# Matmuls of a constant in TensorE's waits, and a finer cut of the last weight, at the end of an attention-plus-FFN decode step

## The chip, the cores and the metric

The kernel runs on one core of one Trainium2 chip. The metric is the device time of one execution in microseconds; lower is better. Three runs of the kernel before gave 1332.01, 1332.43 and 1332.98 us, a median of 1332.43 us.

## The reference

Four sequences decode one token each. A modulation vector is made from `c`, then comes attention over a cache of 4096 keys and values for 32 heads of 128, then a feed-forward block:

```python
mod = (_silu(c) @ w_mod).reshape(4, 6, 1, -1)      # sa, ca, ga, sb, cb, gb
h = _layernorm(x) * (1 + ca) + sa
q = (h @ wq) per head;  scores = einsum(q, k_cache) * 128 ** -0.5
o = einsum(softmax(scores), v_cache)
x = x + ga * (o @ wo)
h = _layernorm(x) * (1 + cb) + sb
x = x + gb * (_silu(h @ w1) @ w2)                   # w1: 512 x 1792, w2: 1792 x 512
```

All values are float32. The two caches alone are 537 MB, and every byte of them is used once.

## The kernel before, in words

The work is cut into N = 64 steps: 16 pairs of heads (t) times 4 sequences (b). One step n loads 4 MB of keys and 4 MB of values into buffers that rotate through one pool of five (tag "kv"), which the weights `wo`, `w1` and `w2` use too. All these loads are issued by SyncE (line 71, in `fetch` and `load`), in the order in which the program writes them, so they stand in one queue.

In a step GpSimd and VectorE multiply the keys with the query (L216), VectorE sums them (L221) and takes the maximum (L225), TensorE transposes the maximum (L229), ScalarE takes the exponential into `pz` (L247), and TensorE multiplies `pz` with the values in `pv` (L260): 16 matmuls with 32 weight columns and 512 moving columns, of which four stand side by side on the four column groups of the array. The trace shows each of these as two instructions (32 in a step).

The schedule is manual: each engine does its instructions in the order of the program. The end of the kernel is this. In the last step (n = 63) SyncE is given the loads of the last values, of the second half of `wo` (four pieces, L319), of `w1` (three pieces, L334) and of `w2` (four pieces, L335). TensorE does the first half of the output projection, `project(0, NH)` (L336, matmuls on L294, 64 of them with 128 moving columns), and then `pv(63)` (L337), for which the last values must have landed. Then follow, one after the other and each waiting for the last:

- `finish_a` and `finish_b` (L340, L341): VectorE copies the sums (L269), TensorE reduces them (L271, L276), VectorE divides;
- `project(NH, NT)` (L342): 64 more matmuls on L294;
- `x1` and the layer norm on VectorE (L345 to L347), with two small matmuls (L165, L169) and one square root on ScalarE (L171) inside it, then the transpose `h2T` (L131);
- the first FFN matmul into `ph` (L352): for each of four slices k of `w1` four matmuls, one a column group, with 448 moving columns;
- SiLU: tanh on ScalarE (L126), a product on VectorE (L127) and the transpose `hidT` (L131);
- the second FFN matmul into `pf` (L362): 14 slices i of `w2`, four matmuls each with 128 moving columns;
- two products and sums on VectorE (L367, L368) and the store (L371).

`psum(..., "q", 2)` is a pair of PSUM banks that `make_qb` (L196) uses in turn for the spread queries; `ph` takes one of them. `ident` is a 128x128 identity, and `qs` holds the scaled queries, written once at the start.

Of the kernel before, what the change touches and what calls it, by code (L numbers as in the profile page):

```python
# [17 lines left out]
def kernel(  # L18
# [13 lines left out]
    nc = tc.nc  # L32
    P = 128
    B, H, S, Dh = kc.shape
    D = x.shape[2]
# [10 lines left out]
    NI = F // P  # L46
# [13 lines left out]
    def psum(shape, tag, bufs):  # L60
        return ps.tile(shape, F32, tag=tag, name=tag, bufs=bufs)
# [5 lines left out]
    w2v = w2.rearrange("(p i) d -> p i d", p=P)  # L67

    def fetch(t, src, *cuts):
        for lo, hi in zip(cuts, cuts[1:]):  # L70
            nc.sync.dma_start(t[:, lo:hi], src[:, lo:hi])

    def load(name, shape, src, *cuts):
        t = kv.tile(shape, F32, tag="kv", name=name)
        fetch(t, src, *(cuts or (0, shape[1])))
        return t
# [3 lines left out]
    def load_k(n):  # L80
        t, b = divmod(n, B)
        src = kc[b, HP * t : HP * (t + 1)].rearrange("h (p j) d -> (h p) j d", p=HALF)
        kt[n] = load(f"k{n}", [P, NJ, Dh], src)

    def load_v(n):
        t, b = divmod(n, B)
        src = vc[b, HP * t : HP * (t + 1)].rearrange("h (p j) d -> (h p) j d", p=HALF)
        vt[n] = load(f"v{n}", [P, NJ, Dh], src)
# [14 lines left out]
    ident = const.tile([P, P], F32, name="ident")  # L103
# [25 lines left out]
    def transposed(src, m, name):  # L129
        d = const.tile([P, m, W], F32, name=name)  # L130
        nc.vector.transpose(d, src.rearrange("p (c k) -> p k c", k=m))  # L131
        return d
# [23 lines left out]
    def layernorm_mod(dst, src, sh, sc1):  # L156
        def t(tag, n):
            return work.tile([P, n], F32, tag=tag, name=tag, bufs=1)

        st, mv, dm, q, r, u = t("st", 6), t("mv", 2), t("dm", 1), t("lnq", 1), t("lnr", 2), t("lnu", P)  # L160
        nc.vector.bn_stats(st, src)
        nc.vector.bn_aggr(mv, st)
        avgm = avg.rearrange("p g w -> p (g w)")
        pm = psum([P, 1], "mx", 2)
        nc.tensor.matmul(pm, avgm, mv[:, 0:1], start=True, stop=True)  # L165
        nc.vector.tensor_sub(dm, mv[:, 0:1], pm)
        nc.vector.scalar_tensor_tensor(q, dm, dm, mv[:, 1:2], op0=ALU.mult, op1=ALU.add)
        pq = psum([P, 1], "mx", 2)
        nc.tensor.matmul(pq, avgm, q, start=True, stop=True)  # L169
        nc.vector.scalar_tensor_tensor(u, src, pm, sc1, op0=ALU.subtract, op1=ALU.mult)  # L170
        nc.scalar.activation(r[:, 0:1], pq, AF.Sqrt, bias=epst)  # L171
        nc.vector.reciprocal(r[:, 1:2], r[:, 0:1])
        nc.vector.scalar_tensor_tensor(dst, u, r[:, 1:2], sh, op0=ALU.mult, op1=ALU.add)
# [7 lines left out]
    CW = 4 * Dh  # L181
    pq = [psum([P, CW], "q", 2) for _ in range(2)]
    for k in range(NK):
        for ch in range(H * Dh // CW):
# [3 lines left out]
                start=k == 0, stop=k == NK - 1,  # L188
            )
    qs = const.tile([P, 2, CW], F32, name="qs")  # L190
# [5 lines left out]
    def make_qb(t):  # L196
        p = psum([P, B, Dh], "q", 2)
        for b in range(B):
            for i in range(HP):
                ch, u = divmod(HP * t + i, CW // Dh)  # L200
                j, g = divmod(ch, G)
                nc.tensor.matmul(  # L202
                    p[HALF * i : HALF * (i + 1), b, :],
                    ident[:, W * g + b : W * g + b + 1].to_broadcast([P, HALF]),
                    qs[:, j, u * Dh : (u + 1) * Dh],
                    start=True, stop=True,
                )
        qb[t] = p
        qw[t] = work.tile([P, B, Dh], F32, tag="qw", name=f"qw{t}")
        nc.scalar.activation(qw[t], p, AF.Copy)  # L210
# [3 lines left out]
    def mult(eng, src, n, lo, hi):  # L214
        t, b = divmod(n, B)
        eng.tensor_mul(  # L216
            kt[n][:, lo:hi, :], kt[n][:, lo:hi, :], src[t][:, b : b + 1, :].to_broadcast([P, hi - lo, Dh])
        )

    def red(n, lo, hi):  # L220
        nc.vector.tensor_reduce(sc[n][:, lo:hi], kt[n][:, lo:hi, :], axis=AX.X, op=ALU.add)  # L221

    def rowmax(n):
        nm[n] = work.tile([P, 1], F32, tag="rm", name=f"rm{n}", bufs=3)
        nc.vector.tensor_reduce(nm[n], sc[n], axis=AX.X, op=ALU.max)  # L225
# [27 lines left out]
    def pv(n):  # L253
        t, b = divmod(n, B)
        if b == 0:
            po[t] = psum([P, JJ * Dh], "po", 2)
        o = W // 2 - JJ - JJ * b
        for j in range(NG):
            g = j % G
            nc.tensor.matmul(  # L260
                po[t][W * g : W * (g + 1), :],
                pz[n % NP][:, j * W + o : (j + 1) * W + o],
                vt[n][:, JJ * j : JJ * (j + 1), :].rearrange("p j d -> p (j d)"),
                start=(b == 0 and j < G), stop=(b == B - 1 and j >= NG - G),
            )

    def finish_a(t):
        o = work.tile([P, JJ, Dh], F32, tag="o", name="o")
        nc.vector.tensor_copy(o, po[t].rearrange("p (j d) -> p j d", j=JJ))  # L269
        d = psum([P, 1 + HP, B], "small", 1)  # L270
        nc.tensor.matmul(d[:, 0, :], blk, rs[t], start=True, stop=True)  # L271
        for i in range(HP):
            for r in range(HP):
                for j in range(JJ):
                    s = i * W // 2 + j
                    nc.tensor.matmul(  # L276
                        d[HALF * i : HALF * (i + 1), 1 + r, :], o[:, j, r::HP], sel[:, s : s + JJ * (B - 1) + 1 : JJ],
                        start=j == 0, stop=j == JJ - 1,
                    )
        sm[t] = d  # L280

    def finish_b(t):
        rd = work.tile([P, 1, B], F32, tag="rd", name="rd")
        nc.vector.reciprocal(rd, sm[t][:, 0:1, :])
        nc.vector.tensor_mul(oz[:, t, :, :B], sm[t][:, 1 : 1 + HP, :], rd.to_broadcast([P, HP, B]))  # L285
# [4 lines left out]
    def project(lo, hi):  # L290
        for t in range(lo, hi):
            for r in range(HP):
                for g in range(G):
                    nc.tensor.matmul(  # L294
                        accp[W * g : W * (g + 1), :], oz[:, t, r, :],
                        wot[t // NH][:, t % NH, r, g * P : (g + 1) * P],
                        start=(t == 0 and r == 0), stop=(t == NT - 1 and r == HP - 1),
                    )

    NH = NT // 2  # L300
    make_qb(0)
    load_v(0)
    for n in range(N):
        t, b = divmod(n, B)
        if n + 1 < N - 3:
            load_k(n + 1)
            load_v(n + 1)
        elif n == N - 4:
            load_k(N - 3)
            load_k(N - 2)  # L310
            load_k(N - 1)
        elif n == N - 3:
            load_v(N - 3)
            load_v(N - 2)
        elif n == N - 2:
            wot.append(load("wo0", [P, NH, HP, D], wov[:, :NH]))
        else:
            load_v(n)
            wot.append(load("wo1", [P, NH, HP, D], wov[:, NH:], 0, NH // 2, 3 * NH // 4, NH - 1, NH))  # L319
        sc[n] = work.tile([P, NJ], F32, tag="sc", name=f"sc{n}", bufs=3)  # L320
        mult(nc.gpsimd, qw, n, 0, NA)
        mult(nc.vector, qb, n, NA, NJ)
        if n >= B and b == 0:
            finish_a(t - 1)
        red(n, NA, NJ)
        if n >= B and b == 0:
            finish_b(t - 1)
        red(n, 0, NA)
        rowmax(n)
        bmax(n)  # L330
        negmax(n)
        softexp(n)
        if n == N - 1:
            w1t = load("w1", [P, NK, F], w1v, 0, 2, 3, 4)  # L334
            w2t = load("w2", [P, NI, D], w2v, 0, 8, 12, 13, 14)  # L335
            project(0, NH)  # L336
        pv(n)  # L337
        if b == 1 and t + 1 < NT:
            make_qb(t + 1)
    finish_a(NT - 1)  # L340
    finish_b(NT - 1)  # L341
    project(NH, NT)  # L342

    x1 = const.tile([P, P], F32, name="x1")
    nc.vector.tensor_mul(x1, ga, accp)  # L345
    nc.vector.tensor_add(x1, x1, xg)
    layernorm_mod(hg, x1, sb, cb1)  # L347
    h2T = transposed(hg, NK, "h2T")
    ph = psum([P, FG], "q", 2)
    for k in range(NK):  # L350
        for g in range(G):
            nc.tensor.matmul(  # L352
                ph[W * g : W * (g + 1), :], h2T[:, k, :], w1t[:, k, g * FG : (g + 1) * FG],
                start=k == 0, stop=k == NK - 1,
            )
    hid = const.tile([P, FG], F32, name="hid")
    silu2(hid, ph, FG)
    hidT = transposed(hid, NI, "hidT")
    pf = psum([P, P], "po", 2)
    for i in range(NI):  # L360
        for g in range(G):
            nc.tensor.matmul(  # L362
                pf[W * g : W * (g + 1), :], hidT[:, i, :], w2t[:, i, g * P : (g + 1) * P],
                start=i == 0, stop=i == NI - 1,
# [32 lines left out]
```

## Time and profile before

| what | us |
|---|---|
| median of three runs (lowest, highest) | 1332.43 (1332.01, 1332.98) |
| the profiled execution | 1334.54 |
| span of the profiled execution, first to last instruction | 1332.5 |
| VectorE busy in it | 976.2 (73%) |
| TensorE matmuls busy | 504.9 (38%) |
| GpSimd busy | 435.2 (33%) |
| ScalarE busy | 75.7 (6%) |
| DMA rate over the span | 426 GB/s |

The profile is of one execution. "PE" is TensorE's matmuls, "PEld" its weight loads, which lie beside them, "DVE" is VectorE, "ACT" ScalarE, "SPq" the queue of SyncE that issues DMAs. The granted clock (PEclk) is the share of full speed that TensorE was given in a stretch: 1.0 is 2.4 GHz and 0.50 is 1.2 GHz, and a value between them is a stretch with some of each. Ends of matmuls are modelled, starts are recorded. A few matmul records can be missing.

### The profile page before, as it was taken

What the parts mean: (1) busy time and instruction counts of PE and PEld (TensorE: products, weight loads), DVE (VectorE), ACT (ScalarE), POOL (GpSimd) and SP (SyncE); (2) the same over time, 40 slices, a digit from 0 to 9 for tenths busy, and PEclk for the clock granted to TensorE, in tenths of its full rate; (3) what the DMA queues carried; (4) which work ended last, traced back from release to release, by engine and by line L of the source; (5) the groups of instructions that cost most, each with busy time, mean ns of one, the idle gap of its engine ahead of it and who ended that gap; (6) DMA issues with size and microseconds to landing.
All of it is one profiled execution on the core that took longest, in us unless ns stands there. A gap on an engine that the chain in (4) does not pass through costs nothing.

```text
span 1332.5 us, 8833 instructions
## 1 busy us (share of the span) xinstructions
PE 504.9 (38%) x3576; PEld 181.2 (14%) x3576; DVE 976.2 (73%) x468; ACT 75.7 (6%) x289; POOL 435.2 (33%) x79
## 2 busy tenths in 40 slices
PE   3244324433442533443343233334333333433157
PEld 2011101110110111101011110101111011101024
DVE  1487787788778778777877877777787787778851
ACT  1100000000000000000000000000000000000000
POOL 1244234324323423432442343243234234324600
PEclk9666677666656666656666676576666556666677
DMA  9999999999999999999999999999999999999997
GB/s 407 427 430 433 426 436 428 429 435 426 433 432 429 433 427 435 430 430 432 427 435 429 428 434 429 432 430 431 432 429 430 430 432 432 431 428 433 431 414 288
DMA packets 22376, 567.87 MB, mean 426 GB/s; under 512 B 2448, under 2 KB 2496, under 8 KB 5056
## 3 DMA queue, kind: packets, MB, share of 16 engines
q1 hardware_dynamic: 22160, 567.29, 99.3%
q8 instruction: 28, 0.46, 0.1%
q14 instruction: 12, 0.10, 0.0%
q0 software_dynamic: 128, 0.01, 0.0%
q10 hardware_dynamic: 48, 0.01, 0.0%
HBM read 567.30 MB, written 0.01 MB: 426 GB/s over the span
## 4 chain that ended last, share of the span: by engine, by line
DMA 48%; DVE 35%; PE 10%; issue 4%; ACT 2%; DVEq 0%; ACTq 0%
DMA k<-in_A_k_cache_dram 45%; DVE sc L221 20%; DVE k L216 13%; PE po L260 8%; DMA v<-in_A_v_cache_dram 2%; ACT pz L247 2%; PE mx L229 1%; DMA wm<-in_w_mod_dram 1%; DVE o L269 1%; DVE rm L225 1%; DVE nm L236 1%; PE acc L294 0%; PE po L362 0%; PE q L352 0%; DVE oz L285 0%
## 5 line engine op out<-in xcount | busy, mean ns | idle before, releaser
L216 POOL TENSOR_TENSOR k<-k,qw 128x3072 f32<-128x3072 f32 x64 | 429.7, 6715 | 827.9 <-DMA k<-in_A_k_cache_dram 786.7
L221 DVE TENSOR_REDUCE sc<-k 128x40 f32<-128x5120 f32 (+1 forms) x128 | 560.8, 4413 | 5.2
L216 DVE TENSOR_TENSOR k<-k,q 128x5120 f32<-128x5120 f32 x64 | 351.2, 5488 | 245.9 <-DMA k<-in_A_k_cache_dram 188.2
L260 PE MATMUL po<-v,pz 128*32 128x512 f32 x2048 | 371.5, 892 | 103.0 <-ACT pz L247 77.1
L229 PE MATMUL mx<-ident,rm 128*128 128x128 f32 x64 | 28.5, 445 | 641.4 <-DVE rm L225 641.4
L260 PEld LDWEIGHTS po<-v,pz 128*32 128x32 f32 x2048 | 82.6, 155 | 349.0 <-issue 256.3
L247 ACT ACTIVATE pz<-sc,nm 64x64 f32<-64x64 f32 x128 | 44.2, 345 | 1054.1 <-DVE nm L236 1052.5
L229 PEld LDWEIGHTS mx<-ident,rm 128*128 128x128 f32 x64 | 11.6, 181 | 676.2 <-issue 648.2
L236 DVE TENSOR_REDUCE nm<-mx 64x1 f32<-64x64 f32 x128 | 28.4, 222 | 45.9 <-PE mx L229 43.9
L276 PE MATMUL small<-sel,o 128*64 128x4 f32 x512 | 43.0, 231 | 46.6 <-DVE o L269 46.6
L276 PEld LDWEIGHTS small<-sel,o 128*64 128x64 f32 x512 | 41.6, 190 | 48.0 <-DVE o L269 48.0
L247 ACT ACTIVATION_READ_ACCUMULATOR pz<-sc,nm 64x1 f32 x128 | 23.6, 185 | 0.0
L269 DVE COPY o<-po 128x512 f32<-128x512 f32 x16 | 11.0, 684 | 16.2 <-PE po L260 16.2
L202 PE MATMUL q<-qs,ident 128*64 128x128 f32 x256 | 17.5, 279 | 0.0
L225 DVE TENSOR_REDUCE rm<-sc 128x1 f32<-128x64 f32 x64 | 14.1, 220 | 2.2
L202 PEld LDWEIGHTS q<-qs,ident 128*64 128x64 f32 x256 | 13.6, 136 | 14.5 <-issue 14.5
L210 ACT ACTIVATE qw<-q 128x512 f32<-128x512 f32 x16 | 9.6, 597 | 105.5 <-PE q L202 105.5
L146 PE MATMUL q<-wm,csT 128*32 128x128 f32 x192 | 7.5, 322 | 17.2 <-DVE csT L131 13.5
L186 PE MATMUL q<-wq,hT 128*32 128x512 f32 x64 | 10.1, 790 | 9.5 <-DMA wq<-in_A_wq_dram 9.5
L294 PE MATMUL acc<-wo,oz 128*32 128x128 f32 x256 | 11.7, 369 | 0.4 <-DMA wo<-in_A_wo_dram 0.4
L294 PEld LDWEIGHTS acc<-wo,oz 128*32 128x32 f32 x256 | 11.2, 154 | 0.7 <-issue 0.6
L146 PEld LDWEIGHTS q<-wm,csT 128*32 128x32 f32 x192 | 6.2, 129 | 17.9 <-DVE csT L131 13.5
(57 smaller groups left out, 63.8 us busy)
## 6 DMA issues: line engine op xcount, KB each, us to landing
k<-in_A_k_cache_dram SPq DMA_DIRECT2D x64, 4096.0 KB, 36.0
v<-in_A_v_cache_dram SPq DMA_DIRECT2D x64, 4096.0 KB, 30.3
wq<-in_A_wq_dram SPq DMA_DIRECT2D x2, 4096.0 KB
wm<-in_w_mod_dram SPq DMA_DIRECT2D x2, 3072.0 KB, 10.1
wo<-in_A_wo_dram SPq DMA_DIRECT2D x1, 4096.0 KB
wo<-in_A_wo_dram SPq DMA_DIRECT2D x1, 2048.0 KB
w<-in_B_w_dram SPq DMA_DIRECT2D x1, 2048.0 KB, 23.7
w<-in_B_w_dram SPq DMA_DIRECT2D x1, 1792.0 KB
```

Of the source, the lines that this page charges most:

```text
L146: nc.tensor.matmul(p[W * g : W * (g + 1), u, :], csT[:, k, :], wmt[k // 2][:, k % 2, o : o + P], start=k == 0, stop=k == NK - 1,)
L202: nc.tensor.matmul(p[HALF * i : HALF * (i + 1), b, :], ident[:, W * g + b : W * g + b + 1].to_broadcast([P, HALF]), qs[:, j, u * Dh : (u + ...
L216: eng.tensor_mul(kt[n][:, lo:hi, :], kt[n][:, lo:hi, :], src[t][:, b : b + 1, :].to_broadcast([P, hi - lo, Dh]))
L221: nc.vector.tensor_reduce(sc[n][:, lo:hi], kt[n][:, lo:hi, :], axis=AX.X, op=ALU.add)
L225: nc.vector.tensor_reduce(nm[n], sc[n], axis=AX.X, op=ALU.max)
L229: nc.tensor.transpose(p, nm[n].to_broadcast([P, P]), ident)
L236: nc.vector.tensor_reduce(t[h], nm[n][h, h], axis=AX.X, op=ALU.max, negate=True)
L247: nc.scalar.activation(w[:, :, o + i * W // 2 : o + i * W // 2 + JJ], sc[n][h].rearrange("p (g j) -> p g j", j=JJ), AF.Exp, bias=nm[n][h], ...
L260: nc.tensor.matmul(po[t][W * g : W * (g + 1), :], pz[n % NP][:, j * W + o : (j + 1) * W + o], vt[n][:, JJ * j : JJ * (j + 1), :].rearrange ...
L269: nc.vector.tensor_copy(o, po[t].rearrange("p (j d) -> p j d", j=JJ))
L276: nc.tensor.matmul(d[HALF * i : HALF * (i + 1), 1 + r, :], o[:, j, r::HP], sel[:, s : s + JJ * (B - 1) + 1 : JJ], start=j == 0, stop=j == ...
L294: nc.tensor.matmul(accp[W * g : W * (g + 1), :], oz[:, t, r, :], wot[t // NH][:, t % NH, r, g * P : (g + 1) * P], start=(t == 0 and r == 0 ...
```

## The change

A helper `busy(m)` issues m matmuls that multiply the first half of `qs` (128 x 512) with the whole identity into a PSUM tile of its own, `idle`, which nobody reads. Nineteen of them are put at six places of the end: 6 between the first half of the projection and `pv(63)`, 2 before the second layer norm, 3 behind it, 2 behind slice 1 and 2 behind slice 2 of the first FFN matmul, and 4 between the two FFN matmuls. The load of `w2` is cut at other slices: 0, 4, 8, 11, 13, 14, which makes five pieces (six numbers), where there were four.

```diff
     NH = NT // 2
+    idle = []
+
+    def busy(m):
+        if not idle:
+            idle.append(psum([P, CW], "q", 2))
+        for _ in range(m):
+            nc.tensor.matmul(idle[0], ident, qs[:, 0, :], start=True, stop=True)
+
     make_qb(0)
...
         if n == N - 1:
             w1t = load("w1", [P, NK, F], w1v, 0, 2, 3, 4)
-            w2t = load("w2", [P, NI, D], w2v, 0, 8, 12, 13, 14)
+            w2t = load("w2", [P, NI, D], w2v, 0, 4, 8, 11, 13, 14)
             project(0, NH)
+            busy(6)
         pv(n)
...
     nc.vector.tensor_add(x1, x1, xg)
+    busy(2)
     layernorm_mod(hg, x1, sb, cb1)
     h2T = transposed(hg, NK, "h2T")
+    busy(3)
     ph = psum([P, FG], "q", 2)
     for k in range(NK):
         for g in range(G):
...
                 start=k == 0, stop=k == NK - 1,
             )
+        if k in (1, 2):
+            busy(2)
+    busy(4)
     hid = const.tile([P, FG], F32, name="hid")
```

## Rows read from the trace of the kernel before

**Rows 1.** The chain that ended last, in order of time: start, us, what.

```profile
1267.96 30.29 DMA v<-in_A_v_cache_dram
...
1305.74 1.88 PE small L276 x32
...
1329.16 0.30 DVE y L367
```

**Rows 2.** The end by stretches: us, busy time of each engine, PEclk, DMA share, GB/s.

```profile
1288.60:1294.90 6.30, 6.30 (x128) 6.06 (x128) 0.15 (x1) 2.14 (x5) 0.00 (x0) 0.57 0.98 415
1294.90:1298.39 3.49, 0.03 (x4) 0.03 (x1) 0.00 (x0) 0.00 (x0) 0.00 (x0) 0.87 0.91 365
1298.39:1305.00 6.61, 6.61 (x34) 1.72 (x34) 0.01 (x1) 0.00 (x0) 0.00 (x0) 0.55 1.04 417
...
1307.55:1312.92 5.37, 5.36 (x130) 5.09 (x128) 0.35 (x2) 0.00 (x0) 0.00 (x0) 0.68 1.03 428
...
1316.96:1321.87 4.91, 4.91 (x32) 1.29 (x32) 0.00 (x0) 0.23 (x1) 0.00 (x0) 0.65 0.79 325
...
1324.16:1329.10 4.94, 4.93 (x112) 4.64 (x112) 0.00 (x0) 0.00 (x0) 0.00 (x0) 0.65 0.05 18
1329.10:1332.50 3.40, 0.00 (x0) 0.00 (x0) 0.58 (x2) 0.00 (x0) 0.00 (x0) 0.87 0.01 2
```

**Rows 3.** Timeline of TensorE's matmuls: start, us, what, idle time before and its releaser.

```profile
1298.39 6.54 PE L260 MATMUL po<-v,pz 128*32 128x512 f32 x32 [3.46 <-DMA v<-in_A_v_cache_dram]
...
1314.29 0.35 PE L165 MATMUL mx<-mv,avg 128*128 128x1 f32 x2 [1.37 <-DVE mv L162]
...
1316.96 4.91 PE L352 MATMUL q<-w,h2T 128*32 128x448 f32 x32 [1.37 <-DVE h2T L131]
1324.16 4.93 PE L362 MATMUL po<-w,hidT 128*32 128x128 f32 x112 [2.29 <-DVE hidT L131]
```

**Rows 4.** Timeline, weight loads of two earlier and later pv steps: one row each four.

```profile
1270.77 0.13 PEld L260 LDWEIGHTS po<-v,pz 128*32 128x32 f32 x4 [0.29 <-issue]
1271.20 0.13 PEld L260 LDWEIGHTS po<-v,pz 128*32 128x32 f32 x4 [0.30 <-issue]
...
1300.07 0.23 PEld L260 LDWEIGHTS po<-v,pz 128*32 128x32 f32 x4 [0.62 <-issue]
1300.92 0.23 PEld L260 LDWEIGHTS po<-v,pz 128*32 128x32 f32 x4 [0.62 <-issue]
```

**Rows 5.** Groups of instructions by line and form, whole execution: busy us, mean ns.

```profile
L260 PE MATMUL po<-v,pz 128*32 128x512 f32 x2048 | 371.5, 892 | 103.0 <-ACT pz L247 77.1 <-DMA v<-in_A_v_cache_dram 21.9 <-issue 4.0
L229 PE MATMUL mx<-ident,rm 128*128 128x128 f32 x64 | 28.5, 445 | 641.4 <-DVE rm L225 641.4
L202 PE MATMUL q<-qs,ident 128*64 128x128 f32 x256 | 17.5, 279 | 0.0
L271 PEld LDWEIGHTS small<-rs,blk 128*128 128x128 f32 x32 | 4.8, 188 | 14.5 <-issue 14.5
```

**Rows 6.** SyncE's issues of the weights w1 and w2 between 1296 and 1300 us.

```profile
L71 SPq DMA_DIRECT2D w<-in_B_w_dram x3: 856/1172/1175, 1295.5 to 1298.3; - x3
```

**Rows 7.** DMA issues of the same stretch: KB each, us from issue to landing.

```profile
w<-in_B_w_dram SPq DMA_DIRECT2D x1, 2048.0 KB, 23.7
w<-in_B_w_dram SPq DMA_DIRECT2D x2, 896.0 KB
```

**Rows 8.** The DMA's last microseconds, by stretches as in rows 2.

```profile
1325.00:1326.00 1.00, 1.00 (x26) 0.99 (x22) 0.00 (x0) 0.00 (x0) 0.00 (x0) 0.50 0.10 33
1326.00:1327.00 1.00, 1.00 (x25) 0.99 (x20) 0.00 (x0) 0.00 (x0) 0.00 (x0) 0.50 0.00 0
```

**Rows 9.** Timeline of all engines: SyncE's weight issues, and VectorE's last use of `q`.

```profile
1273.04 5.49 DVE L216 TENSOR_TENSOR k<-k,q 128x5120 f32<-128x5120 f32 x1
...
1283.97 23.54 SPq L71 DMA_DIRECT2D w<-in_B_w_dram  x7
...
1329.80 0.67 SPq L371 DMA_DIRECT2D out_dram<-y  x2
```

## The prediction

> **What bounds the kernel now.** I read the page's slices of clock and DMA first: the DMA works at its rate until the last of the forty slices, so the time in front of the last values is a matter of bytes, and the change leaves the bytes alone. So I went to the chain that ended last, for what comes behind them. The last values land at 1298.25 us, 30.29 after 1267.96 [rows 1]; what TensorE and VectorE do after that, some 34 us, is the only part that the change can touch. Third, the end by stretches, for the clock: the last `pv` ran at a granted clock of 0.55, the second half of the projection at 0.68, and both FFN matmuls at 0.65 [rows 2]. The reader should see that each of these began at or fell to 1.2 GHz after TensorE had been idle or nearly so, and rose to 2.4 GHz after it had streamed for some time. Fourth, TensorE's timeline, for the idle time ahead of each stretch: 3.46 us for the values, 1.37 us ahead of the norm's first matmul, 1.37 us ahead of the first FFN matmul, 2.29 us ahead of the second [rows 3]. The change fills these.
>
> **What full clock can give back.** A stretch that streams all the time at a mean clock c would take c times its time at full clock, so it gives back (1 - c) of it [rows 2]: `pv` 6.61 x 0.45 = 2.97 us; the projection 5.37 x 0.32 = 1.72; the first FFN matmul 4.91 x 0.35 = 1.72; the second 4.94 x 0.35 = 1.73. Together 8.14 us. The 1.88 us of the reduction [rows 1] ran at full clock already and give nothing.
>
> **What one matmul of the constant costs.** The trace has none of 128 weight columns by 512 moving ones. The nearest in length is `pv`: its weight loads, four to a pass, come 0.43 us apart at full clock and 0.85 us apart at half [rows 4]. Four column groups share that pass; is a pass over the whole array as long? In L202 two groups share it, 16 passes of 128 columns in each of 16 calls (256 instructions), with 17.5/16 = 1.09 us a call, 0.137 us a pair [rows 5]; a pair of 512 columns would be four times that at most, 0.55. So neither two groups nor four makes a pass much shorter or longer, and I take 0.43. Every ordinary float32 matmul stands twice in the trace (8 matmuls a call, 16 instructions in L202), so one matmul of the constant is two passes: 0.85 us at full clock, 1.71 at half. The lower bound is one pass, 0.43: the transposes with the same identity are 64 instructions in 64 steps [rows 5]. The upper bound adds a weight load in the open to every pass: 0.188 us for 128 columns [rows 5], 1.23 us in all. I take 0.85, since `pv`'s loads lie beside the pass before.
>
> **What lies beside other work and what on the path.** TensorE does its instructions in order, so whatever of a fill lasts longer than the idle time delays the real matmul behind it, and the VectorE work behind that.
> - busy(6): 5.12 us where 3.46 were idle. It holds `pv` back, and with it the copy on VectorE: +1.66.
> - busy(2) ahead of the norm: 1.71 against 1.37, and the matmul of the means and its subtraction on VectorE wait: +0.34. `x1` itself does not wait, as it needs only the projection.
> - busy(3): 2.56 against 1.37; the first FFN matmul waits though `h2T` is there: +1.19.
> - busy(2) twice inside the first FFN matmul: no idle time stands between its slices (one row of 4.91 us busy in 4.91 [rows 2]), so all four matmuls are on the path: +3.41. This is the dearest item. It would cost nothing if `w1` were late there. But the first part of `w2`, 2048 KB, was issued at 1298.3 [rows 6] and landed 23.7 us later [rows 7], at 1322.0, and at 325 to 417 GB/s [rows 2] those bytes take 5.0 to 6.5 us, so the last of `w1`, ahead of it in the queue, landed at 1317 or before (an estimate). By the sums here, slice 2 is needed at about 1318.8 and slice 3 at 1321.2 in the changed kernel.
> - busy(4): 3.41 against 2.29 of SiLU; the second FFN matmul waits: +1.12.
>
> Sum of the fills 7.72 us, given back 8.14 us: **0.42 us faster than the profiled execution**, a span of 1332.1. The second FFN matmul would begin 1.3 us later than now (7.72 of fills less 2.97 + 1.72 + 1.72 given back), at about 1325.5, and take 1.73 less.
>
> **The pieces of w2.** They are five, not six. All 3.67 MB still follow `w1` in the one queue. The extra issue takes at most the 1.175 us of the longest in [rows 6]; SyncE has nothing to do from 1307.51 (1283.97 + 23.54) until the store at 1329.80 [rows 9], so this is hidden; without that cover it would cost itself. The first slices would be there about 2.5 us sooner (half of the 5.0), but the second FFN matmul waits for `hidT` [rows 3], not for them: 0. The last bytes land in the stretch from 1325 to 1326 [rows 8]; the last slice is needed at about 1328.4. That leaves 2 to 3 us, and this is what is late next if the path shrinks.
>
> **The PSUM bank.** `idle` takes the bank that `ph` had, last read for step 59; `ph` moves to the one that VectorE reads for step 63, from 1273.04 on for 5.49 us [rows 9], 38 us before `ph` needs it. No wait: 0; without that lead, at most those 5.49 us.
>
> **Against the median.** The profiled execution took 1334.54 us, 2.11 more than the median. The clock is a draw: all 64 `pv` steps have the same matmuls and took 371.5/64 = 5.80 us busy on average [rows 5], against 6.54 in the last [rows 3]. If none of the 2.11 us is a colder clock at the end, the sum stands, -0.42; if all of it is, the kernel before had 2.11 us less to give back in those runs, and the change costs +1.69. I take the middle, +0.6: **1333.0 us**. For this kernel a measurement can tell about 0.2% (2.7 us) from nothing, so this is no change.
>
> **The rivals.**
> - *The fills cost half or less.* If the matmul of the constant goes in one pass, as the transposes do, fills of 2.56, 0.85, 1.28 and 1.71 us fit inside their idle times, and only the two inside the first FFN matmul cost, 1.71 us. Then 6.4 us would be saved, but the last bytes of `w2` stop it: landed at about 1325.6, two short rounds of matmuls (0.2) and the end of 3.40 us [rows 2] give a span of 1329.2, 3.3 less. Against the median, with half of the 2.11 us gone, that is -2.2: 1330.2. For: the fills would fit the gaps closely. Against: every ordinary matmul of the trace has two passes. The Trainium skill (TensorE: Matmul & The Clock Gate, "Wait — 56ns, not 53.3ns?") gives 215.7 ns from start to start for 512 columns at full clock, in its own measurements; by that figure, an estimate, the nineteen take 4.1 us in all, four of them (0.86 us) on the path, and the time is this rival's. The rows here say 0.43 us a pass and two passes, so I give this little. Chance 0.12, of which 0.05 beyond 0.2%.
> - *Weight loads in the open: slower.* `pv` shows loads of 32 columns beside a running pass. If loads over all 128 columns can't start until the pass that uses the whole array is done, each of the 38 passes gets 0.188 us more [rows 5]: 7.1 us, all on the path, as the fills are longer than their cover already: 1333.0 + 7.1 = 1340.1. It decides from 0.055 us a pass on (2.1 us over 38). For: nothing in the trace loads a whole array beside a long pass. Against: `pv` loads the same column group while it streams, without a gap. Chance 0.08.
> - *The constant does not hold the clock.* Then nothing is given back and each matmul takes 1.71 us: 32.4 us less the covers of 8.49 is 24 us slower, 1356. Against: `pv` streams with weights that are mostly zero too, and the clock rises in it. Chance 0.03.
> - Something else: 0.04.
>
> **How the numbers follow.** My forecast has 0.73; its own range goes from -0.42, less 0.7 for the modelled ends of five idle times, to +1.69, plus about 1 if one stretch still starts cold: 1331.3 to 1335.1. The range over cases takes in most of the first rival: 1330.2 to 1335.6; the slower rivals, the rest and the edges, some 0.18, are left out. Faster by over 0.2%: 0.05 from the first rival and 0.02 from the forecast's edge, 0.07. Slower: 0.08 + 0.03 + 0.04 of edges and the rest, 0.15. Within: 0.78.
>
> **What would show it.** Right: from 1295 us on the granted clock stays near 1.0; fills with weight loads 0.43 us apart; `pv` starts about 1.7 us after its values landed and lasts 3.6 us; the first FFN matmul is split and lasts 6.6 us from start to end; no wait for `w1` or `w2`. Wrong: passes 0.2 us apart, or 0.6; a clock of 0.5 within the fills; a second FFN matmul that waits for the DMA; a SiLU that ends behind busy(4).

## The result, and the profile after

The changed kernel took 1336.38 us (median of 8 runs, 1335.77 to 1338.58), the kernel before in the same comparison 1332.62 us (8 runs, 1331.86 to 1333.43). The ratio is 1.003, with a 95% interval of 1.002 to 1.004: slower by 3.8 us, where no change was forecast, and 0.8 us above the stated range.

The clock did what was hoped. The end of the changed kernel by stretches, with the columns of [rows 2]: the fill ahead of `pv`, `pv`, the second half of the projection, the norm with its two fills, the first FFN matmul with its two, the fill behind it, and the second FFN matmul.

```profile
1295.05:1300.39 5.34, 5.34 (x14) 2.19 (x12) 0.00 (x0) 0.00 (x0) 0.00 (x0) 1.00 0.97 391
1300.39:1304.10 3.71, 3.71 (x35) 1.07 (x34) 0.00 (x0) 0.00 (x0) 0.00 (x0) 1.00 1.05 420
1306.65:1310.35 3.70, 3.70 (x131) 3.50 (x129) 0.35 (x2) 0.00 (x0) 0.00 (x0) 1.00 0.99 414
1310.35:1316.01 5.66, 5.07 (x18) 2.33 (x22) 2.62 (x10) 1.54 (x2) 0.00 (x0) 1.00 1.01 411
1316.01:1323.26 7.25, 7.25 (x41) 2.09 (x41) 0.00 (x0) 0.00 (x0) 0.00 (x0) 1.00 0.78 315
1323.26:1326.89 3.63, 3.63 (x12) 1.44 (x16) 1.56 (x2) 0.54 (x1) 0.00 (x0) 1.00 0.18 72
1326.89:1330.15 3.26, 3.19 (x112) 2.92 (x112) 0.00 (x1) 0.00 (x0) 0.00 (x0) 1.00 0.00 0
```

The granted clock is 1.00 throughout, where [rows 2] had 0.55 to 0.68. TensorE is busy for almost all of it, and that is the trouble: the chain that ended last, in order of time, now runs through the matmuls of the constant (L307).

```profile
1295.12 5.35 PE q L307 x12
1300.46 3.61 PE po L260 x32
...
1306.72 3.63 PE acc L294 x128
1310.35 1.91 PE q L307 x4
...
1313.33 2.68 PE q L307 x6
1316.01 1.64 PE q L363 x16
1317.65 1.91 PE q L307 x4
1319.56 0.89 PE q L363 x8
1320.45 1.91 PE q L307 x4
1322.37 0.89 PE q L363 x8
1323.26 3.63 PE q L307 x8
1326.89 3.24 PE po L376 x112
```

Four instructions of it (two matmuls) take 1.91 us, eight 3.63, twelve 5.35: 0.86 us a matmul, and 0.19 us once for each of these fills; the fill of three (2.68) has 0.10. The six fills sum to 17.39 us. In the profile of before the same chain went from the values to `pv` [rows 1] with none of this.

### The profile page after: what moved, and what is told of

Read it like the earlier page. It is cut to its first block, busy times and chain, and to the rows that moved or that the text cites. A ratio compares the mean times of both kernels' runs of the same rounds, so it can differ in the third digit from the quotient of the medians.

```text
span 1333.9 us, 8910 instructions
## 1 busy us (share of the span) xinstructions
PE 510.9 (38%) x3614; PEld 183.5 (14%) x3614; DVE 976.2 (73%) x468; ACT 75.7 (6%) x289; POOL 435.1 (33%) x79
## 4 chain that ended last, share of the span: by engine, by line
DMA 46%; DVE 36%; PE 11%; issue 5%; ACT 2%; DVEq 0%; ACTq 0%
DMA k<-in_A_k_cache_dram 43%; DVE sc L221 21%; DVE k L216 13%; PE po L260 7%; DMA v<-in_A_v_cache_dram 3%; ACT pz L247 2%; PE q L307 1%; PE mx L229 1%; DMA wm<-in_w_mod_dram 1%; DVE o L269 1%; PE acc L294 1%; DVE rm L225 1%; DVE nm L236 1%; PE q L363 0%; PE po L376 0%
## 5 line engine op out<-in xcount | busy, mean ns | idle before, releaser
L260 PE MATMUL po<-v,pz 128*32 128x512 f32 x2048 | 364.7, 877 | 99.0 <-ACT pz L247 77.1
L269 DVE COPY o<-po 128x512 f32<-128x512 f32 x16 | 10.9, 684 | 14.7 <-PE po L260 14.7
L307 PE MATMUL q<-qs,ident 128*128 128x512 f32 x38 | 17.9, 608 | 0.0
```

The lines of the kernel that those rows point to most:

```text
L260: nc.tensor.matmul(po[t][W * g : W * (g + 1), :], pz[n % NP][:, j * W + o : (j + 1) * W + o], vt[n][:, JJ * j : JJ * (j + 1), :].rearrange ...
L307: nc.tensor.matmul(idle[0], ident, qs[:, 0, :], start=True, stop=True)
```

## The experiments

All ratios are to the kernel before, run beside each kernel on the same chip. Its medians in the four comparisons lie between 1332.62 and 1333.20 us, so medians from different comparisons can be set side by side to some 0.6 us. Three theories stood: (1) the fills that outlast their waits are the loss, measured against a kernel before that in most executions had less to give back than in the profiled one; (2) the profiled execution of before is typical; (3) the cut of `w2`, or the longer program, costs.

### e1 and e11: the kernel before, two more profiles

No edit.

> The kernel before, unchanged, for a second profile of it. Theory 1 (the draw): the one profiled execution of before was colder at its end than most, so that the change had less to give back than it seemed. Then this profile spans about 1330.5 us (the median of 1332.6 less the 2.1 between time and span), and at least two of the four stretches (pv, the second half of the projection, the two FFN matmuls) have a granted clock well above the 0.55, 0.68, 0.65 and 0.65 of the first profile. Theory 2 (the draw is no part of it): the four clocks are within 0.05 of those, and the span is 1332 or more, or it is shorter for another reason.

> The kernel before, unchanged, for a third profile. Theory 1 (the clock of the end is drawn anew in each execution): a span between 1329.8 and 1332.5, and a set of four clocks unlike either of the first two profiles. Rival (the first profile was an odd one, the second is the rule): the four clocks within 0.05 of the second profile.

Measured: the second profile spans 1330.3 us (median of 10 runs 1332.35, ratio 0.9996, interval 0.9987 to 1.0005), the third 1329.4 (one run, 1331.47), 0.4 below the span that I had stated for it. The same stretches as [rows 2], the second profile and then the third: `pv`, projection, first and second FFN matmul.

```profile
1298.36:1303.52 5.16, 5.16 (x34) 1.42 (x34) 0.01 (x1) 0.00 (x0) 0.00 (x0) 0.71 1.04 414
1306.07:1309.84 3.77, 3.70 (x130) 3.43 (x128) 0.35 (x3) 0.00 (x0) 0.00 (x0) 1.00 1.01 421
1313.82:1318.72 4.90, 4.90 (x32) 1.11 (x32) 0.00 (x0) 0.22 (x1) 0.00 (x0) 0.65 1.01 420
1322.09:1326.90 4.81, 4.76 (x112) 4.50 (x112) 0.00 (x0) 0.00 (x0) 0.00 (x0) 0.67 0.25 94
```

```profile
1298.03:1301.70 3.67, 3.67 (x33) 1.20 (x33) 0.00 (x0) 0.00 (x0) 0.00 (x0) 1.00 1.04 414
1304.28:1308.90 4.62, 3.91 (x130) 3.37 (x128) 0.35 (x2) 0.00 (x0) 0.00 (x0) 1.00 1.04 429
1312.91:1317.85 4.94, 4.91 (x32) 1.19 (x32) 0.00 (x0) 0.22 (x1) 0.00 (x0) 0.65 1.02 429
1321.83:1326.05 4.22, 3.68 (x112) 2.87 (x112) 0.00 (x0) 0.00 (x0) 0.00 (x0) 1.00 0.33 126
```

The same program had `pv` at 0.55, 0.71 and 1.00, the projection at 0.68, 1.00 and 1.00, and the second FFN matmul at 0.65, 0.67 and 1.00; the first FFN matmul had 0.65 in all three. Theory 1 holds in both and theory 2 falls: two clocks rose in the second profile, three in the third, and the first profile was the slowest of three. TensorE's idle time ahead of `pv` differed as well: 3.46, 2.91 and 1.79 us, as in the second and third profile the last four instructions of the first half of the projection came later (see the last section). That it alone sets the clock of `pv` is not shown: in e2 2.95 us went with 0.68, in e7 4.17 us with 0.68 too. What stands next is in the waits of TensorE's timeline, in the second profile and in the third:

```profile
1322.09 4.76 PE L362 MATMUL po<-w,hidT 128*32 128x128 f32 x112 [3.37 <-DMA w<-in_B_w_dram]
```

```profile
1321.83 1.96 PE L362 MATMUL po<-w,hidT 128*32 128x128 f32 x64 [4.01 <-DMA w<-in_B_w_dram]
1324.24 1.75 PE L362 MATMUL po<-w,hidT 128*32 128x128 f32 x48 [0.45 <-DMA w<-in_B_w_dram]
```

In [rows 3] this matmul waited for `hidT`; here it waits for `w2`, and the chain that ended last in the second profile goes through that load, not through the first FFN matmul:

```profile
1298.29 23.67 DMA w<-in_B_w_dram
1321.96 0.14 issue
1322.09 4.80 PE po L362 x112
```

So where the clock of `pv` and of the projection comes back, the kernel before already ends behind its last weight, and little is left to win.

### e2: the cut of w2 alone

```diff
-            w2t = load("w2", [P, NI, D], w2v, 0, 8, 12, 13, 14)
+            w2t = load("w2", [P, NI, D], w2v, 0, 4, 8, 11, 13, 14)
```

> Only the cut of w2, no matmul of the constant. Theory 1 (the fills are the whole loss): no difference, within 0.6 us of before. Theory 3 (the cut costs: one more issue and finer pieces make the last bytes late): 1 to 2 us slower than before, and the DMA's last bytes 1 us later than in the profile of before.

Measured: 1333.20 us, ratio 0.9999 (0.9990 to 1.0008). Nothing: theory 3 falls for the cut. Its profile (span 1331.5) is one more draw of nearly the same program, between the first two of before: `pv` at 0.68, the projection at 0.74, both FFN matmuls at 0.66, and here the second of them waited for `hidT`, as in [rows 3]:

```profile
1322.73 4.92 PE L362 MATMUL po<-w,hidT 128*32 128x128 f32 x112 [2.29 <-DVE hidT L131]
```

### e3: without the fills inside the first FFN matmul

```diff
-        if k in (1, 2):
-            busy(2)
```

> The changed kernel without the four matmuls of the constant inside the first FFN matmul; the other fifteen and the cut of w2 stay. Theory 1: the two inner fills took 1.91 us each in the chain of the changed kernel, so 3.8 us go: 1332.5, no difference from before, with the whole end at a clock of 1.0. The last bytes of w2 would then be next: the second FFN matmul ends no earlier than they land. Theory 3 (the cut) or a loss by loading of longer code: most of the loss stays, 1334.5 or more.

Measured: 1333.22 us, ratio 0.9999 (0.9991 to 1.0008); its profile spans 1330.2 us. Those four matmuls carry nearly all of the loss, 3.2 us of 3.8 by the two medians. The second FFN matmul in its timeline:

```profile
1321.63 1.95 PE L374 MATMUL po<-w,hidT 128*32 128x128 f32 x64
1324.01 0.86 PE L374 MATMUL po<-w,hidT 128*32 128x128 f32 x24 [0.42 <-DMA w<-in_B_w_dram]
1325.28 1.07 PE L374 MATMUL po<-w,hidT 128*32 128x128 f32 x24 [0.41 <-DMA w<-in_B_w_dram]
```

It begins 5.2 us sooner than in the changed kernel (1.3 of that were there at the start of `pv`) and then waits for pieces of `w2`; what else would be saved is lost there.

### e4: short fills

```diff
-            busy(6)
+            busy(4)
...
-    busy(2)
+    busy(1)
     layernorm_mod(hg, x1, sb, cb1)
...
-    busy(3)
+    busy(1)
...
-        if k in (1, 2):
-            busy(2)
-    busy(4)
+    busy(2)
```

> Short fills: 4, 1, 1, none inside the first FFN matmul, and 2, eight in all, so that none outlasts its wait by the 0.86 us that one takes and the 0.19 of a turn. Theory 1: nothing of the fills is on the path, the clock stays at or near 1.0 from 1295 us on, and the end is set by the last bytes of w2: about 1331.7, some 0.9 below before, at the edge of what 5 rounds tell. If short fills do not hold the clock: a stretch with 0.5 to 0.7, and 1333 or more.

Measured: 1332.21 us (11 runs, 1331.68 to 1332.38), ratio 0.9995 (0.9986 to 1.0004): 4.2 us below the changed kernel, and not to be told from before, though its 11 runs lie within 0.7 us where the 33 of before spread over 3.1. The whole end in one stretch, and the matmuls that waited for `w1` or `w2`:

```profile
1294.90:1326.07 31.17, 25.61 (x360) 13.09 (x358) 5.22 (x15) 2.09 (x3) 0.00 (x0) 1.00 0.88 360
```

```profile
1316.83 0.96 PE L363 MATMUL q<-w,h2T 128*32 128x448 f32 x8 [1.23 <-DMA w<-in_B_w_dram]
...
1321.81 1.08 PE L374 MATMUL po<-w,hidT 128*32 128x128 f32 x32 [0.64 <-DMA w<-in_B_w_dram]
1323.69 0.86 PE L374 MATMUL po<-w,hidT 128*32 128x128 f32 x24 [0.80 <-DMA w<-in_B_w_dram]
1325.01 1.06 PE L374 MATMUL po<-w,hidT 128*32 128x128 f32 x24 [0.46 <-DMA w<-in_B_w_dram]
```

Full clock all the way with eight matmuls of the constant in place of nineteen; the last three fills end before what they wait for is there, and TensorE waits for `w1` and `w2` four times (and once, 0.23 us, for `wo`).

### e5: the inner fills doubled

```diff
         if k in (1, 2):
-            busy(2)
+            busy(4)
```

> The changed kernel with four matmuls of the constant, not two, behind slice 1 and behind slice 2 of the first FFN matmul. Theory 1 (each of them is on the path, 0.86 us): in the chain of the changed kernel a fill of four took 3.63 us and one of two 1.91, so two times 1.72, 3.4 us more than the changed kernel: about 1339.8. Rival (the inner fills stand where the first FFN matmul would wait for w1 or the second for w2 anyway): 1 us more or less.

Measured: 1339.47 us, ratio 1.0053 (1.0038 to 1.0068), 3.1 us more than the changed kernel by the medians; the spans of the two profiles differ by 3.5 (1337.4 and 1333.9). Theory 1: each is on the path at full price.

### e6: the same nineteen, half as wide

```diff
-            nc.tensor.matmul(idle[0], ident, qs[:, 0, :], start=True, stop=True)
+            nc.tensor.matmul(idle[0][:, : CW // 2], ident, qs[:, 0, : CW // 2], start=True, stop=True)
```

> The changed kernel with the same nineteen matmuls in the same places, each over 256 moving columns, not 512. This makes the prediction's first rival true (a matmul of the constant at half the cost). Theory 1 (the length of the fills is the loss, not their number or place): 0.43 us each and 0.19 a turn; the fills of 6, 2, 3 and 4 fit their waits but for some 0.1 to 0.3 us, and the inner two cost about 1.05 us each where TensorE has to wait for w1 and w2 by then. So the last bytes of w2 set the end: 1332.0 to 1332.6, no difference from before. Rival (the number of turns counts, or less streaming lets the clock fall): 1334 or more, or a stretch at 0.7 or less.

Measured: 1332.45 us, ratio 0.9997 (0.9989 to 1.0006), the clock at 1.00 from the first fill to the end:

```profile
1296.18:1326.30 30.12, 27.03 (x382) 17.15 (x380) 5.23 (x15) 2.09 (x3) 0.00 (x0) 1.00 0.88 359
...
1323.96 0.86 PE L376 MATMUL po<-w,hidT 128*32 128x128 f32 x24 [0.82 <-DMA w<-in_B_w_dram]
1325.24 1.07 PE L376 MATMUL po<-w,hidT 128*32 128x128 f32 x24 [0.42 <-DMA w<-in_B_w_dram]
```

The two inner fills take 1.06 us each, and the second FFN matmul waits for `w2` behind them all the same, so their time is taken up by that wait. Number and place are the changed kernel's, and so is the length of the program, with which the rest of theory 3 falls; only the width is not. This is the prediction's first rival made true, and it gives no difference either, not the 2.2 us that I had put on it.

### e7 and e8: without the first fill, and the first fill alone

e7 takes out `busy(6)`; e8 takes out all the others.

> The changed kernel without the six matmuls ahead of the last pv. In the changed kernel they made pv start 2.4 us after its values had landed, and pv took 3.6 us from its start. Prediction's account (cost 1.66, given back 2.97): without them it is 1.3 us slower than the changed kernel, about 1337.7. Theory 1 (most executions are like the second profile of before, in which pv took 5.1 us without any fill): 2.4 less and 1.5 more, 0.9 us faster than the changed kernel, about 1335.5.

> Only the six ahead of pv, and the cut of w2; no other fill. Theory 1: pv ends about 0.9 us later than in the second profile of before, but that one waited 1.1 us for the first piece of w2 at the end, so nearly all of it is hidden: no difference from before, 1332.5 to 1333.5. Prediction's account: 1.3 us faster than before, 1331.5, with a pv that ends earlier than in either profile of before.

Measured: e7 1337.00 us, ratio 1.0028 (1.0017 to 1.0040); e8 1333.14 us, ratio 1.0002 (0.9993 to 1.0011). e8 came out as theory 1 had it, and not as my account of the first fill: in its profile VectorE's copy behind `pv` starts at 1304.02 us, against 1303.51 in the second profile of before. e7 does not separate the two accounts: its interval overlaps that of the changed kernel and holds both expected times. In its profile `pv` ran 5.34 us at a clock of 0.68, from 1298.04 on. What the first fill is worth beside the others stays open, about 1 us either way.

### e9 and e10: fewer bytes of w2

```diff
-            w2t = load("w2", [P, NI, D], w2v, 0, 4, 8, 11, 13, 14)
+            w2t = load("w2", [P, NI, D], w2v, 0, 4, 8)
...
-                pf[W * g : W * (g + 1), :], hidT[:, i, :], w2t[:, i, g * P : (g + 1) * P],
+                pf[W * g : W * (g + 1), :], hidT[:, i, :], w2t[:, i % 8, g * P : (g + 1) * P],
```

> The short fills of e4, and only the first 8 of the 14 slices of w2 are loaded; the second FFN matmul uses slices 0 to 5 again in place of 8 to 13, so it does the same number of matmuls, and the output is not the reference's. Theory 1 (with short fills the last bytes of w2 set the end, and TensorE has time left): 1.57 MB less to load, some 3.5 us, so the waits for w2 in the second FFN matmul go, but for one that ends when the first 8 slices are there; it would end about 3 us sooner: 1329.2. Rival (the end is set by TensorE's work alone): 1332.2, as with all of w2.

> The changed kernel with the same cut: only 8 slices of w2 loaded, slices 0 to 5 used twice, so the output is not the reference's. Theory 1 (in the changed kernel the fills have taken the place of the last bytes of w2 as what sets the end): no gain from the bytes left out, 1336 to 1336.8. Rival (it is still the DMA): about 3 us faster, 1333.4.

Measured: with short fills 1329.92 us, ratio 0.9977 (0.9968 to 0.9987), 2.3 us below e4; with the changed kernel's fills 1336.28 us, ratio 1.0025 (1.0016 to 1.0034), the changed kernel's own time. So the last bytes end the first, and TensorE's own fills end the second; behind `pv` no matmul waits for a weight in e10's timeline, nor in the changed kernel's. e9 gained 2.3 rather than 3 us. In its profile the second half of the projection took 5.11 us, against 3.70 at full clock, so that one execution at least did not hold the clock everywhere; the last wait for `w2` is the 0.63 us ahead of the last 80 instructions:

```profile
1305.11 5.11 PE L294 MATMUL acc<-wo,oz 128*32 128x128 f32 x128
...
1321.87 2.39 PE L374 MATMUL po<-w,hidT 128*32 128x128 f32 x80 [0.63 <-DMA w<-in_B_w_dram]
```

## Why the prediction was wrong

Starts of the same instructions (us), from the timelines:

| | before, first | second (e1) | third (e11) | changed | e4 |
|---|---|---|---|---|---|
| `pv` | 1298.39 | 1298.36 | 1298.03 | 1300.39 | 1298.49 |
| copy L269 | 1304.99 | 1303.51 | 1301.73 | 1304.10 | 1302.19 |
| `x1` | 1312.98 | 1309.83 | 1308.93 | 1310.42 | 1308.94 |
| subtraction L166 | 1314.68 | 1311.53 | 1310.62 | 1312.42 | 1310.64 |
| first FFN matmul | 1316.96 | 1313.82 | 1312.91 | 1315.94 | 1312.92 |
| tanh L126 | 1321.94 | 1318.79 | 1317.89 | 1323.32 | 1317.85 |
| second FFN matmul | 1324.16 | 1322.09 | 1321.83 | 1326.82 | 1320.08 |
| last product | 1329.16 | 1326.92 | 1326.05 | 1330.15 | 1326.14 |
| span | 1332.5 | 1330.3 | 1329.4 | 1333.9 | 1329.9 |

**The cost of one matmul of the constant: right.** Two passes, 0.43 us apart at full clock, 0.86 us in all. That the weight loads lie beside the pass before was right too, as its timeline shows:

```profile
1296.44 0.19 PEld L307 LDWEIGHTS q<-qs,ident 128*128 128x128 f32 x1 [0.24 <-issue]
1296.87 0.19 PEld L307 LDWEIGHTS q<-qs,ident 128*128 128x128 f32 x1 [0.24 <-issue]
```

This agrees with the Trainium skill (TensorE: Matmul & The Clock Gate, "Part 2: What happens when you issue a matmul"), by which the weights of the next matmul load while one runs. The 215.7 ns for 512 columns that the Trainium skill gives (TensorE: Matmul & The Clock Gate, "Wait — 56ns, not 53.3ns?") is not what float32 shows here: 430 ns for each of two passes. The second rival fell with these rows, as did the cost that the first one rests on, and the third (the constant does not hold the clock) with the granted clock of 1.00.

**What full clock gives back, against the first profile: right to 0.5 us.** From start to start in the table, `pv` 2.89 (2.97 forecast), the projection 1.67 (1.72), the second FFN matmul 1.67 (1.73); the first FFN matmul 1.42 (1.72), counting its two fills at 1.91 us each.

**The fills on the path: right in kind, 0.9 us short.** Differences of the changed kernel to the first profile, and in brackets the forecast: `pv` starts 2.00 later (1.66); from `x1` to the subtraction 0.30 more (0.34); from there to the first FFN matmul 1.24 (1.19); the two fills inside it 3.82 (3.41); from tanh to the second FFN matmul 1.28 (1.12). Summed, 8.64 against 7.72. With the 0.5 us less given back, and 0.41 us more from the last product to the end of the span (3.75 against 3.34; e4 has 3.76, and no run explains it), that makes the 1.8 us between the -0.42 us forecast and the +1.4 us that the two profiled spans show (1333.9 - 1332.5). Most of the 0.9 is the 0.19 us of each fill, which the sum did not have: once at `pv`, twice in the first FFN matmul and once behind it.

**The step that failed: "I take the middle".** It left the sum with most of the 8.14 us of clock that it had found in one cold execution. The prediction said: "if all of it is, the kernel before had 2.11 us less to give back in those runs, and the change costs +1.69". That was the nearer case. The second and third profiles, 2.2 and 3.1 us shorter than the first in span, have warmer clocks in the same stretches and wait for `w2` at the end. Against the second, which is close to the median of its ten runs, the changed kernel is 3.6 us longer in span, close to the 3.8 measured. In the table: against it, the changed kernel has lost 2.0 us at `pv`, is 0.6 behind at `x1`, 0.9 at the subtraction, 2.1 at the first FFN matmul, 4.5 at the tanh and 4.7 at the second FFN matmul, and gets back 1.5 there.

Term by term, against that second profile, the clock gives back 4.35 us (`pv` 1.44, the projection nothing, the FFN matmuls 1.41 and 1.50), where the prediction had 8.14 less half of 2.11, some 7.1. The fills cost 7.58 us, close to the 7.72 forecast, because the last one stands in part where the second profile waits for `w2`; 0.37 us are at the end. So the mis-sized term is what the clock gives back: a usual execution had lost less of it, and where it had lost little, the last bytes of `w2` set the end instead.

That the profiled execution was so cold was bad luck: its 1334.54 us is as much as the slowest of the 33 runs of before beside e1. To price four stretches by one execution was not luck. The one row that speaks of the draw (5.80 us for a mean `pv` against 6.54 [rows 3, 5]) pointed the right way; the sum still let the one profile stand for half of it. The signs that the prediction listed could not show this, as all of them lie in the changed kernel's trace. Most came true there: the clock, the passes 0.43 us apart, a `pv` of 3.6 us, no wait for `w1` or `w2`.

**The range.** The forecast's own range ended at 1335.1 (+1.69 and 1 us), the stated one, over all cases, at 1335.6. Counted from the first profile, the errors are 1.1 us of the draw (1.69 for 0.6) and 1.8 of the fills and the rest of that sum, 2.9 of the 3.4 us between 1333.0 and 1336.4, and together they took the time past it.

## What to carry to other kernels

A matmul of no use kept the clock up in most of these profiles (not all the way in e9's), but TensorE does it in order: give it less than the shortest wait that it fills. Between matmuls that have no wait between them it costs its full time (e3, e5), unless a later wait takes that up (e6). Before pricing a cold clock by one profile, take a second profile of the same kernel: here three of them had three sets of clocks, and one made a poor base for a sum. And ask first what would end the kernel if the cold stretch were free: here it was the last bytes of a weight, 2 to 3 us below the profile that I worked from, and two of three profiles had reached them already.

## What the runs showed that I had not expected

A fill over the whole array between matmuls on four column groups costs 0.19 us beyond its passes, whatever its length: two, four and six matmuls in the changed kernel, and in e6, with half the columns, 1.06 us for two and 2.79 us for six, which leave about 0.2. The fill ahead of the norm's matmul, which is over the whole array too, has 0.10 from start to start (1310.28 to 1312.10 us). That the change of column groups is the reason fits this, but no run tried it by itself.

In 11 of the 13 profiles TensorE stood still ahead of the last four instructions of the first half of the projection, for 0.66 to 1.68 us, and the profile shows nothing that it waited for; in the first profile of before and in e7's it did not. The changed kernel:

```profile
1294.70 0.41 PE L294 MATMUL acc<-wo,oz 128*32 128x128 f32 x4 [0.79 <-issue]
```

In the kernel before this lies inside the wait for the values; with the fill behind it, it is on the path. A transfer of the instruction queue falls between 1292 and 1294 us in the changed kernel's trace:

```profile
q8 instruction: 1, 0.02, 3.2%
```

All 11 profiles with the pause have one between 1290 and 1294 us, and the next between 1301 and 1303. The two without the pause have theirs between 1280 and 1281 and between 1296 and 1298, and none in between. So these instructions may have been on their way; no run moved the transfers, and the cause stays open.
